# A drain instruction on GpSimd's queue, ahead of the first small expert slot of an attention and mixture-of-experts kernel

## The chip, the cores and the metric

One core of a Trainium2 chip runs the whole program. The metric is the device time of one execution in microseconds (us); lower is better. The core's engines are TensorE (PE, with its weight loads as PEld), VectorE (DVE), ScalarE (ACT), GpSimd (POOL) and SyncE (SP); each works through a queue of instructions of its own, in order.

## The reference, cut to what matters

Attention over 8 batches, 8 heads, 576 tokens and 64 columns with rotary positions, and then a mixture of experts in which each of the 4608 tokens goes to the one expert with the highest gate logit:

```python
attn_out = softmax(rotate(q) @ rotate(k).T / 8) @ v
x = attn_out.transpose(0, 2, 1, 3).reshape(4608, 512)
logits = x @ w_gate
expert_idx = argmax(logits, axis=1)
gate_w = softmax(logits)[arange(4608), expert_idx]
for e in range(8):
    mask = expert_idx == e
    out[mask] = gate_w[mask, None] * (maximum(x[mask] @ w1[e], 0) @ w2[e])
```

## The kernel before, in words

The program has two stages. In the first, which lasts to about 485 us of the span, 32 pairs of heads go through scores, softmax and values in an order that tables at the head of the file set (`PLAN`, `FIRST`, `LAST`). The rows that come out are written to a DRAM buffer (`x_dram`), and the index of every token is scattered to the list of its expert (`xlist`) by indirect DMAs that GpSimd issues (`listed`, line 898).

The second stage works through slots of one expert each. A large slot is 256 tokens, a small slot 128. The number of slots depends on the data, so that both loops stand in nested `tc.If` blocks at the end of the function (lines 1434 to 1441): up to 21 large slots, of which this data uses 17 (`s` from 0 to 16), and up to 8 small ones, of which it uses 6 (`s` from `SB` = 22). `counts` holds the two numbers; every engine loads the second of them at line 1432 and then branches at line 1438.

In a slot, SyncE loads the two weight matrices of the next expert where they change (`reload`), ACT and DVE split them into a high and a low part (`split1`, `split2`), and TensorE multiplies. GpSimd computes nothing in this stage. It only issues the indirect DMAs: in large slots the gathers of rows of a later slot (`gather_pieces`, line 441; for three slots `gather`, line 460), for small slots one gather each (`gather_small`, line 1064), issued as early as the large slots, and in every slot the scatter of finished rows to the output (`out_rows`, line 1198), two for a large slot and one for a small one. The rows wait in a tile `y` with three buffers, which DVE (line 249) or ACT (line 1197) fills.

Where a block of large slots is skipped, its false branch holds, on GpSimd, waits for the landings of all earlier indirect DMAs and one instruction that adds to the semaphores what the skipped DMAs would have added (in the rows it stands as INC_SWDGE_SEM); the same stands in the false branch of the small slots. Behind the last block comes the end of the program, which the rows give line 1544: SyncE waits for all landings, each engine runs a drain and reports to GpSimd, GpSimd runs a drain of its own, takes the four reports and releases all engines; a second such round follows, around a clearing of the semaphores.

`small_slot` is called once per small slot. Its first call of `half` emits the first 12 products on TensorE, and the branch `s == SB` below it is taken for the first small slot alone. Of GpSimd's instructions a small slot has only the scatter at its end.

Of the kernel before, what the change touches and what calls it, by code (L numbers as in the profile page):

```python
# [177 lines left out]
def kernel(  # L178
# [12 lines left out]
    nc = tc.nc  # L191
# [236 lines left out]
    def slot_indices(s):  # L428
        return sib[:, s - SB:s - SB + 1] if s >= SB else gi[s % NG]
# [49 lines left out]
    def take():  # L479

        return pairs.pop(0)

    def give(t):
        pairs.append(t)
# [574 lines left out]
    def blocks(t):  # L1059

        return t.rearrange("p (g q c) -> p g c q", q=P, c=2)
# [7 lines left out]
    def reload(s, which, regs, part=None):  # L1069
        if not regs:  # L1070
            regs.append(reg(s, 1, E - 1))
            regs.append(None if s == 0 else reg(s, 2, 1))
        ev, cv = regs
        kw = {} if cv is None else dict(cond=cv)
        for g in range(FQ) if part is None else [part]:
            if which == 1:
                nc.sync.dma_start(out=r1[g], in_=src1(bass.ds(ev, 1), g, SP0 <= s < SB), **({} if s == SP0 else kw))
            else:
                nc.sync.dma_start(out=r2[g], in_=src2(bass.ds(ev, 1), g), **kw)

    def split(hi, lo, src):
        nc.scalar.copy(out=hi, in_=src)  # L1082
        nc.vector.tensor_tensor(out=lo, in0=src, in1=hi.bitcast(F32), op=ALU.subtract)  # L1083

    def split1(g):
        split(w1h[g], w1l[g], r1[g])

    def split2(g):
        split(w2h[g], w2l[g], r2[g])
# [14 lines left out]
    def quarters(t):  # L1104
        return t.rearrange("p a (b q) -> p (a b) q", q=256)
# [15 lines left out]
    def xturn(s, nj):  # L1121
        src = quarter_rows(rows_of(s))
        ps = take()
        readers[id(ps)] = 2
        for dc in range(DC):
            for j in range(nj):
                nc.tensor.transpose(quarters(ps)[:, dc, j * P:(j + 1) * P], src[:, 4 * j + dc, 0:DQ], ident)
        return ps
# [4 lines left out]
    def xhigh(ps, d2, nj):  # L1133
        sl, w = slice(2 * d2, 2 * d2 + 2), slice(0, nj * P)
        nc.scalar.copy(out=xh[:, sl, w], in_=turned_x(ps)[:, sl, w])

    def xlow(ps, d2, nj):
        sl, w = slice(2 * d2, 2 * d2 + 2), slice(0, nj * P)
        nc.vector.tensor_tensor(out=xl[:, sl, w], in0=turned_x(ps)[:, sl, w], in1=xh[:, sl, w].bitcast(F32),
                                op=ALU.subtract)  # L1140
        if ps is not None:
            both(ps)
# [8 lines left out]
    def relu_parts(hp, w):  # L1151
        hh = hq.tile([P, 2, 256], F32R, name="hh")[:, :, 0:w]
        hl = hq.tile([P, 2, 256], F32R, name="hl")[:, :, 0:w]
        nc.scalar.activation(out=hh, in_=hp, func=AF.Relu)
        nc.vector.scalar_tensor_tensor(out=hl, in0=hp, scalar=0.0, in1=hh.bitcast(F32), op0=ALU.max, op1=ALU.subtract)
        return hh, hl
# [12 lines left out]
    def first_products(fs):  # L1169
        return [(w[dc][:, fs], x[:, dc]) for dc in range(DC) for w, x in ((w1h, xh), (w1l, xh), (w1h, xl))]  # L1170
# [23 lines left out]
    def out_rows(s, t, si, yp, ordered):  # L1194
        y = mp.tile([P, DM], F32, name="y", bufs=3)
        w = weight_of(s, t)
        chained_emit(lambda: nc.scalar.mul(y, yp, w) if t else ts(y, yp, w, ALU.mult), ordered)
        sc = nc.gpsimd.indirect_dma_start(  # L1198
            out=out, out_offset=bass.IndirectOffsetOnAxis(ap=si[:, t:t + 1], axis=0),
            in_=y, in_offset=None, bounds_check=NT - 1, oob_is_err=False)  # L1200
        tc.declare_no_dep(sc.ins, group="out", reason="every row is written once")
        tc.add_to_no_dep_group("out", sc.ins)

    def small_slot(s, last):


        def half(h, at):
            t = take()
            hp = t[:, 0]
            todo = first_products(slice(h * 512, h * 512 + 512))  # L1210
            for i, (w, x) in enumerate(todo):
                nc.tensor.matmul(hp, lhsT=x[:, 0:P], rhs=w, start=(i == 0), stop=(i == len(todo) - 1))
                for f in at.get(i, ()):
                    f()
            return t

        def held(hp):
            hs = mp.tile([P, 512], F32, name="hs", bufs=2)
            nc.scalar.copy(out=hs, in_=hp[:, 0])
            give(hp)  # L1220
            return hs

        def turned(hs):

            tp = take()
            for b in range(FQ):
                nc.tensor.transpose(tp[:, 0, b * P:(b + 1) * P], blocks(hs)[:, b // 2, b % 2], ident)
            return tp

        def rounded(tp):  # L1230
            hh, hl = (t.rearrange("p a (b q) -> p (a b) q", q=P) for t in relu_parts(quarters(tp)[:, 0:2], 256))
            give(tp)
            return [(hh[:, 2 * g:2 * g + 2], hl[:, 2 * g:2 * g + 2]) for g in range(2)]

        def next1(d):
            if not last:
                split1(d)

        hs, hp = [], half(0, {})
        if s == SB:  # L1240
            split2(0)
            split2(1)
            hs.append(held(hp))
            split2(2)
            split2(3)
        else:
            for g in range(1, FQ):
                split2(g)
            hs.append(held(hp))
        parts = []  # L1250

        def first_half():
            tp = turned(hs[0])
            if s > SB:
                next1(0)
            parts.extend(rounded(tp))
            if s == SB:
                next1(0)

        hp = half(1, {5: [first_half]})  # L1260
        next1(1)
        hs.append(held(hp))
        if not last:
            reload(s + 1, 2, regs_of[s])
        ps = None if last else xturn(s + 1, 1)
        yt = take()
        yp = yt[:, 0]

        def second(g):
            hh, hl = parts[g]  # L1270
            for i, (h, w, fi) in enumerate([(hh, w, fi) for fi in range(2) for w in (w2h[g], w2l[g])] +
                                           [(hl, w2h[g], fi) for fi in range(2)]):
                nc.tensor.matmul(yp, lhsT=h[:, fi], rhs=w[:, fi], start=(g == 0 and i == 0),
                                 stop=(g == FQ - 1 and i == 5))

        second(0)
        tp = turned(hs[1])
        if not last:
            xhigh(ps, 0, 1)
            xhigh(ps, 1, 1)  # L1280
            xlow(ps, 0, 1)
            xlow(ps, 1, 1)
            next1(2)
        parts.extend(rounded(tp))
        if not last:
            next1(3)
        for g in range(1, FQ):
            second(g)
        if not last:
            split2(0)  # L1290
        out_rows(s, 0, slot_indices(s), yp, False)
        give(yt)
# [30 lines left out]
    def slot(s, nj):  # L1323
        if s < 3 or s >= NA_MIN:
            chained.clear()
        last = s == SB + NB_MAX - 1
        regs = []
        if s + 1 == S1:
            indices(S1, 2, gi[S1 % NG])
        if s + 1 == S1:  # L1330
            gather(S1, 2)
        if s + 1 >= S1 and s + 2 < SB:
            indices(s + 2, 2, gl[s % 2])
        j = s - S1 - 1
        if 0 <= j < NB_MAX:
            indices(SB + j, 1, sib[:, j:j + 1])
        if 1 <= j <= NB_MAX:
            gather_small(j - 1)
        if not last:
            reload(s + 1, 1, regs)  # L1340
        if nj == 1:
            regs_of[s] = regs
            return keep(lambda: small_slot(s, last))
        hs = []
        mm1(s, hs)
        reload(s + 1, 2, regs)
        xtrans(s + 1)
        mm2(s, hs)
# [199 lines left out]
```

## Time and profile before

| what | value |
|---|---|
| median of 3 runs | 966.09 us (965.85 to 968.06) |
| the profiled execution's own time | 962.38 us |
| span of the profiled execution | 960.6 us |
| time outside the span | 1.78 us |
| granted clock of TensorE, mean | 0.993 |
| TensorE busy | 924.5 us, 96% |
| GpSimd busy | 650.6 us, 68%, 559 instructions |

Times in rows count from the start of the span, in us, and durations in a list by source line are in ns (least, median, most). An engine's name with a q behind it (POOLq, SPq) is its queue: branches, semaphore waits and drains, which are not counted as busy. A time outside the span belongs to the execution but to no instruction.

### The profile page before, as it was taken

Reading aid. Unit: us, or ns where it says so; the run is one execution under the profiler, and the core shown is the slowest. Engines: PE = TensorE matmul, PEld = TensorE weight load, DVE = VectorE, ACT = ScalarE, POOL = GpSimd, SP = SyncE. Lnnn points to the kernel's source line nnn. Section 1 sums busy time; section 2 is a strip of 40 time slices with the busy share of each in tenths; the row PEclk is TensorE's granted clock in tenths of the full one; section 3 lists DMA queues with packets and bytes.
Section 4 is the critical chain, followed back from the end, with each engine's and each line's share of the span. In section 5 each row is a group of like instructions: output and inputs, shape, how many; then the busy total and the mean of one; then the engine's idle time right before and its main releaser. Section 6 shows DMA issues by size and latency. Waiting matters only on the chain.

```text
span 960.6 us, 25200 instructions
## 1 busy us (share of the span) xinstructions
PE 924.5 (96%) x9514; PEld 770.0 (80%) x9514; DVE 754.2 (79%) x1324; ACT 624.7 (65%) x1104; POOL 650.6 (68%) x559
## 2 busy tenths in 40 slices
PE   7899999999999999998899999999999999999994
PEld 6677777777777777776689999999999999996883
DVE  7788878788788878778468677777787788788994
ACT  6887777777777777676454444555455555556883
POOL 2998799999989896976346556767667666553110
PEclk9999999999999999999999999999999999999998
DMA  7785665656647655442711277614416311167970
GB/s 256 231 258 149 188 168 161 174 160 193 183 125 220 173 158 164 140 129 85 233 58 47 76 219 235 196 50 146 148 57 194 97 50 47 44 207 273 383 268 10
DMA packets 65492, 152.61 MB, mean 159 GB/s; under 512 B 18841, under 2 KB 34009, under 8 KB 60368
## 3 DMA queue, kind: packets, MB, share of 16 engines
q1 hardware_dynamic: 55760, 130.67, 44.4%
q0 software_dynamic: 9600, 20.23, 6.7%
q8 instruction: 77, 1.26, 0.6%
q14 instruction: 55, 0.45, 0.2%
HBM read 162.35 MB, written 22.69 MB: 193 GB/s over the span
## 4 chain that ended last, share of the span: by engine, by line
PE 53%; issue 18%; POOL 14%; DVE 6%; ACT 4%; DMA 3%; POOLq 0%; DVEq 0%; SPq 0%; ACTq 0%
PE pb L694 12%; PE pb L605 11%; PE pb L1178 10%; PE pb L1305 9%; POOL xg L441 4%; PE pb L631 4%; DVE PT L563 4%; POOL xt L441 3%; PE pb L736 3%; POOL out_dram L1198 3%; PE pb L699 3%; ACT pn L621 3%; DMA qk<-in_qk_dram 1%; DMA out_dram<-y,gi 1%; ACT PT L563 1%
## 5 line engine op out<-in xcount | busy, mean ns | idle before, releaser
L621 ACT ACTIVATE pn<-pb,negm 128x576 f32<-128x576 f32 x256 | 187.2, 739 | 63.1 <-DVE negm L610 57.2
L610 DVE TENSOR_REDUCE negm<-pb 128x1 f32<-128x576 f32 x288 | 201.4, 747 | 16.9 <-PE pb L605 10.2
L605 PE MATMUL pb<-rK,rX 64*128 64x288 f32 (+1 forms) x960 | 166.2, 310 | 7.5 <-DMA rX<-rQ 4.2
L605 PE MATMUL pb<-rK,rQ 64*128 64x288 f32 (+1 forms) x960 | 166.4, 310 | 3.7 <-DVE lgt L762 0.7
L605 PEld LDWEIGHTS pb<-rK,rX 64*128 64x128 f32 (+1 forms) x960 | 133.4, 181 | 26.4 <-issue 10.2
L694 PE MATMUL pb<-PT,vn 128*64 128x320 f32 (+1 forms) x1024 | 150.2, 412 | 3.8 <-issue 3.4
L1178 PE MATMUL pb<-xh,w1h 128*128 128x256 f32 x544 | 153.8, 283 | 0.0
L1178 PE MATMUL pb<-xh,w1l 128*128 128x256 f32 x544 | 153.7, 283 | 0.0
L1178 PE MATMUL pb<-xl,w1h 128*128 128x256 f32 x544 | 153.7, 283 | 0.0
L605 PEld LDWEIGHTS pb<-rK,rQ 64*128 64x128 f32 (+1 forms) x960 | 133.3, 181 | 12.6 <-DVE PT L563 6.8
L1083 DVE TENSOR_TENSOR w2l<-r,w2h 128x1024 fp32r<-128x1024 f32 x89 | 107.4, 1218 | 30.4 <-ACT w2h L1082 26.0
L441 POOL DMA_INDIRECT xg<-x_dram,gp x64 | 90.9, 1420 | 57.5 <-DVE gp L251 40.0
L563 ACT COPY PT<-pb 128x1024 f32<-128x1024 f32 (+1 forms) x99 | 97.3, 1000 | 35.4 <-PE pb L655 30.3
L441 POOL DMA_INDIRECT xt<-x_dram,gp x56 | 79.5, 1420 | 50.0 <-DVE gp L251 31.3
L694 PEld LDWEIGHTS pb<-PT,vn 128*64 128x64 f32 x1024 | 68.8, 136 | 53.0 <-issue 10.8
L1083 DVE TENSOR_TENSOR w1l<-r,w1h 128x1024 fp32r<-128x1024 f32 x88 | 104.7, 1220 | 2.6 <-ACT w1h L1082 1.9
L1178 PEld LDWEIGHTS pb<-xh,w1h 128*128 128x128 f32 x544 | 106.1, 195 | 0.7
L1178 PEld LDWEIGHTS pb<-xh,w1l 128*128 128x128 f32 x544 | 106.1, 195 | 0.5
L1305 PE MATMUL pb<-w2h,hh 128*128 128x512 f32 x272 | 106.2, 390 | 0.0
L1178 PEld LDWEIGHTS pb<-xl,w1h 128*128 128x128 f32 x544 | 106.1, 195 | 0.0
L1305 PE MATMUL pb<-w2l,hh 128*128 128x512 f32 x272 | 106.0, 390 | 0.0
L1305 PE MATMUL pb<-w2h,hl 128*128 128x512 f32 x272 | 105.9, 389 | 0.0
(227 smaller groups left out, 2021.6 us busy)
## 6 DMA issues: line engine op xcount, KB each, us to landing
r<-in_moe_w_dram SPq DMA_DIRECT2D x136, 512.0 KB
qk<-in_qk_dram SPq DMA_DIRECT2D x31, 1152.0 KB
r<-in_moe_w1q_dram SPq DMA_DIRECT2D x56, 512.0 KB
rX<-rQ SPq DMA_DIRECT2D x128, 144.0 KB
x_dram<-xt SPq DMA_DIRECT2D x8, 1032.0 KB
vn<-in_v_dram SPq DMA_DIRECT2D x32, 256.0 KB
vr<-in_vlast_dram SPq DMA_DIRECT2D x32, 64.0 KB
xlist<-mark SPq DMA_DIRECT2D x3, 408.0 KB
```

What stands on the lines that cost most here:

```text
L441: nc.gpsimd.indirect_dma_start(out=t[:, k], out_offset=None, in_=x_dram.rearrange("n (q w) -> (n q) w", q=4), in_offset=bass.IndirectOffse ...
L563: (nc.scalar.copy if eng == "a" else nc.vector.tensor_copy)(out=o, in_=i)
L605: nc.tensor.matmul(sp[0:m, r, 0:HS], lhsT=st["Q" if r == h else "X"][rows[r], a, cols], rhs=parts(st["K"][rows[r], b])[:, h], start=(a + b ...
L610: nc.vector.tensor_reduce(out=st["negm"][:, j:j + 1], in_=st["S", j][:, :, 0:HS], axis=AX.XY, op=ALU.max, negate=True)
L621: nc.scalar.activation(out=parts(pt), in_=sp[:, :, 0:HS], func=AF.Exp, bias=st["negm"][:, j:j + 1], scale=1.0, accum_out=z)
L631: nc.tensor.transpose(tp[:, r, k * 256 + i * 64:k * 256 + i * 64 + 64], pn[rows[r], i, c:c + P], ident[rows[r], rows[r]])
L694: m = nc.tensor.matmul(to[:, 0:w], lhsT=st["vn"][:, h, kt, :], rhs=st["PT"][:, 4 * h + kt, half * 256:half * 256 + w], start=(kt == 0), st ...
L699: m = nc.tensor.matmul(to[:, 0:w].rearrange("p (i q) -> p i q", i=k), lhsT=vr[n % NVR][:, h], rhs=st["PT"][:, 4 * half:4 * half + k, 576:6 ...
L736: m = nc.tensor.matmul(o[:, r, c * 72:c * 72 + 72], lhsT=st["uT"][rows[r], c * P:(c + 1) * P], rhs=iw[rows[r], n % NP, :], start=True, sto ...
L1083: nc.vector.tensor_tensor(out=lo, in0=src, in1=hi.bitcast(F32), op=ALU.subtract)
L1178: m = nc.tensor.matmul(hp[:, fi], lhsT=w, rhs=x, start=(i == 0), stop=(i == len(todo) - 1))
L1305: m = nc.tensor.matmul(yp[:, t], lhsT=h[:, fi, ts_], rhs=w[:, fi], start=(g == 0 and fi == 0 and i == 0), stop=(g == FQ - 1 and fi == 1 an ...
```

## The change

One instruction is added to GpSimd's queue. In the program's order it stands in the block of the first small slot, behind that block's branch (line 1438) and ahead of the slot's scatter (line 1198, with its register move and its wait). It waits for no semaphore and updates none. On the other four engines, and on GpSimd behind it, instructions and waits are what they were.

```diff
         hs, hp = [], half(0, {})
         if s == SB:
+            nc.gpsimd.drain()
             split2(0)
             split2(1)
             hs.append(held(hp))
```

## Rows read from the trace of the kernel before

**Rows 1.** Stretches: length, busy (instructions) of PE, PEld, DVE, ACT, POOL; clock, DMA, GB/s.
```profile
886.00:947.90 61.90, 60.80 (x296) 50.64 (x294) 58.97 (x65) 50.82 (x68) 8.54 (x6) 1.00 0.72 270
947.90:950.70 2.80, 0.00 (x0) 0.00 (x0) 0.00 (x0) 0.00 (x0) 0.94 (x1) 1.00 0.16 63
950.70:960.60 9.90, 0.00 (x0) 0.00 (x0) 0.00 (x0) 0.00 (x0) 0.00 (x0) 0.52 0.00 0
```

**Rows 2.** Line 1544, instructions between 950 and 951 us.
```profile
L1544 POOLq DRAIN  x1: 9060/9060/9060, 950.7 to 950.7; - x1
```

**Rows 3.** Line 1544, instructions between 951.1 and 959 us, SyncE's drains.
```profile
L1544 SPq DRAIN  x2: 7/10/13, 951.2 to 951.3; - x2
```

**Rows 4.** SyncE's queue after 945 us, whom it waited for (total, times, longest).
```profile
SPq L1544 <- DMA out_dram<-y,sib: 10.8, 1, 10.8
SPq L1544 <- PEq L1544: 9.2, 2, 8.7
```

**Rows 5.** Line 1544, whole span: GpSimd's events and drains, SyncE's events.
```profile
L1544 POOLq EVENT_SEMAPHORE  x4: 17/17/17, 959.8 to 960.5; - x4
L1544 POOLq DRAIN  x3: 51/107/9060, 950.7 to 960.3; - x3
L1544 SPq EVENT_SEMAPHORE  x14: 17/28/28, 950.5 to 960.5; - x14
```

**Rows 6.** Line 1529, the start of the program: GpSimd's drain.
```profile
L1529 POOLq DRAIN  x1: 169/169/169, 0.3 to 0.3; - x1
```

**Rows 7.** GpSimd's groups of indirect DMAs in the whole span.
```profile
L441 POOL DMA_INDIRECT xg<-x_dram,gp x64 | 90.9, 1420 | 57.5 <-DVE gp L251 40.0 <-issue 14.6 <-PE pb L1178 2.9
L441 POOL DMA_INDIRECT xt<-x_dram,gp x56 | 79.5, 1420 | 50.0 <-DVE gp L251 31.3 <-issue 13.1 <-PE pb L1178 5.6
L898 POOL DMA_INDIRECT xlist<-tid,lpi x40 | 45.3, 1133 | 12.0 <-issue 7.4 <-DMA gi<-xlist 3.4 <-DMA x_dram<-xt 0.3
L1198 POOL DMA_INDIRECT out_dram<-y,gi x34 | 40.1, 1180 | 16.5 <-issue 9.1 <-DVE y L249 6.1 <-ACT w2h L1082 0.9
L1064 POOL DMA_INDIRECT xsm<-x_dram,sib x8 | 9.7, 1212 | 2.4 <-issue 2.4
L1198 POOL DMA_INDIRECT out_dram<-y,sib x6 | 9.5, 1579 | 65.8 <-DVE y L249 55.1 <-DVEq L1438 10.7
L460 POOL DMA_INDIRECT xt<-x_dram,gi x4 | 4.7, 1166 | 15.6 <-DVE uT L714 14.7 <-issue 0.9
L460 POOL DMA_INDIRECT xg<-x_dram,gi x4 | 4.6, 1145 | 1.2 <-issue 1.2
```

**Rows 8.** GpSimd's queue at the two false branches (lines 1434 and 1438).
```profile
L1434 POOLq INC_SWDGE_SEM  x1: 2277/2277/2277, 879.2 to 879.2; - x1
...
L1438 POOLq INC_SWDGE_SEM  x1: 2371/2371/2371, 948.1 to 948.1; - x1
```

**Rows 9.** Chain of waits, 868 to 883 us.
```profile
871.27 10.11 DMA out_dram<-y,gi
...
882.07 0.04 POOLq L1438
...
882.15 0.04 POOLq L1198
```

**Rows 10.** GpSimd's timeline, 850 to 961 us.
```profile
872.61 1.00 POOL L1198 DMA_INDIRECT out_dram<-y,gi  x1 [0.31 <-ACT w2h L1082]
886.04 1.70 POOL L1198 DMA_INDIRECT out_dram<-y,sib  x1 [12.44 <-DVE y L249]
898.40 1.70 POOL L1198 DMA_INDIRECT out_dram<-y,sib  x1 [10.65 <-DVE y L249]
```

**Rows 11.** GpSimd's timeline, 474 to 490 us.
```profile
478.21 1.00 POOL L460 DMA_INDIRECT xt<-x_dram,gi  x1 [0.30 <-issue]
479.24 2.37 POOL L1364 TENSOR_TENSOR w1l<-r,w1h 128x1024 fp32r<-128x1024 f32 x1
```

**Rows 12.** Tile y after 880 us, DVE's writes of it.
```profile
L249 DVE TENSOR_SCALAR y<-pb,xsm x6: 751/751/754, 885.0 to 946.8; 128x512 f32<-128x512 f32 x6
```

## The prediction

> **What bounds the kernel now.** TensorE is busy for 96% of the span, so the last place where anything else counts is where TensorE has finished. I therefore read the busy time by stretches first, at the end of the span [rows 1]: up to 947.9 us TensorE is busy for 60.80 of 61.90 us, and the other engines follow it. From there on no engine computes. 2.80 us hold only the issue of the last scatter, and then come 9.90 us in which nothing is busy and no DMA moves anything. The list of the end's instructions says what these 9.90 us are: one drain on GpSimd's queue that starts at 950.7 us and executes for 9060 ns [rows 2], that is to 959.8 us.
>
> Next is the question whether something else would have held the end back anyway. SyncE's waits [rows 4] and its instructions [rows 3, 5] answer it: SyncE waited for the landing of the last scatter, had that by 950.5 us (its first wait for landings is over there, [rows 5]), and had executed its own drain by 951.3 us [rows 3]. From then on it waited 8.7 us; the view puts that down to TensorE's queue, but TensorE had nothing left to do, and SyncE's wait ends when GpSimd, behind its drain, takes the reports (first at 959.8 us, [rows 5]) and releases everyone. So the drain alone sets the end, for all but its first 0.6 us. What follows it, 960.60 - 959.76 = 0.84 us, is the release and the second round.
>
> **What the change adds, and where.** It adds one drain. The chain of waits [rows 9] gives its place: GpSimd's branch into the first small slot is at 882.07 us, the next instruction of the slot at 882.15 us, so the drain starts at about 882.15 us. Queued behind it on GpSimd are the scatter of the first small slot, which now starts at 886.04 us [rows 10] when DVE's y is there, and the five scatters behind that. Ahead of it, the scatters of the last large slot were issued by 873.61 us, and their landings had been waited for in the false branch by 881.38 us [rows 9]. GpSimd stands still for 12.44 us there [rows 10], of which 886.04 - 882.15 = 3.9 us lie behind the drain's start.
>
> *How long the new drain takes.* No row shows a drain in that place. The rows give two ends: 51 to 169 ns for a drain with nothing but a few fills or semaphore instructions ahead of it [rows 5, 6], and 9060 ns for the one at the end, with the whole kernel ahead of it [rows 2]. What lies between the two kinds is the 216 indirect DMAs that GpSimd issued (64 + 56 + 40 + 34 + 8 + 6 + 4 + 4, [rows 7]). The drain at the end can't be waiting for the newest of them: the last scatter had landed by 950.5 us [rows 4, 5] and the semaphore instruction ahead of the drain had ended at 948.1 + 2.37 = 950.5 us [rows 8]. It isn't plain work that lags on GpSimd's cores either: a subtract behind an indirect DMA starts 0.03 us after that DMA's row ends and has an ordinary length [rows 11]. So what the drain executes is either older than the newest work, something that each indirect DMA leaves behind until a drain clears it, or a routine of fixed length.
>
> I take the first: 9060 / 216 = 42 ns for each indirect DMA since the last drain. Then 210 of them are cleared in the middle, at 210 x 42 ns = 8.8 us, from 882.15 to about 891.0 us. The first scatter moves from 886.04 to about 891.1 us, 5 us later, and is issued by 892.8 us, 5.6 us before the second is due at 898.40 us [rows 10]. The cover is GpSimd's own idle time. Nobody reads the output in the kernel; the one who waits for a scatter is DVE, which fills y again when the scatter three slots earlier has landed. DVE's six fills stand 12.36 us apart ((946.8 - 885.0) / 5, [rows 12]), so the fourth, at 922.1 us, needs the first scatter landed; with the slow landing of this stretch, 10.11 us from the issue [rows 9], it has landed at 901.2 us, 21 us in time. Without that cover the 5 us would fall on DVE and then on TensorE. The price of the added drain on the path is therefore 0.
>
> *What goes.* The drain at the end then has 6 scatters ahead of it, 6 x 42 ns = 0.25 us, and the floor of 0.05 to 0.17 us seen for empty ones. It would be over at about 951.0 us, and SyncE's drain, over at 951.3 us [rows 3], is late next. The end moves from 959.76 to about 951.29 us: **8.5 us less**. If the drain keeps a fixed part of a few us besides the 42 ns, it saves less: with half of 9.06 us kept, the drain ends at 955.4 us and 4.4 us go.
>
> *The sum.* Span 960.6 - 8.5 = 952.1 us; with the 1.78 us around it the profiled execution would take 953.9 instead of 962.38 us. The runs shown have a median 3.7 us above that execution, and I put the same 8.5 us on the median: 966.09 - 8.5 = **957.6 us**. Taken alone, this case reaches from 956.0 (the least run lies 0.2 us under the median, and the empty drain may add a few tenths of saving in the release) to 962.0 us (half of the length kept).
>
> **The rule that speaks against it.** The rows show drains of 7 to 13 ns on SyncE [rows 3] and of 51 to 9060 ns on GpSimd [rows 5]. The Trainium skill, "VectorE: DVE Perf Modes", section "The DRAIN you can't avoid", says that the drains from a program's beginning and end are boilerplate of about 12 ns, constant, on all five engines. By that rule the added drain costs 12 ns, the one at the end isn't something to save, and the time stays at 966.1 us. The trace agrees for SyncE and not for GpSimd's row of 9060 ns.
>
> **The rivals.**
>
> *The drain has a fixed length once indirect DMAs have run (chance 0.34).* For it: only one drain with indirect DMAs ahead of it is in the trace, so one length can't tell 42 ns each from 9.06 us at once; the instruction that adds to semaphores also takes much the same in both places, 2277 and 2371 ns, however many DMAs lie between [rows 8]. Against it: nothing that the rows show was open at 950.7 us. Then the middle drain takes 9.06 us, hidden as above, and the one at the end again 9.06 us, since six scatters and a semaphore instruction lie between. The time is 966.1 us.
>
> *The added drain doesn't do what the one at the end does (0.06).* Its queue is empty at 882.15 us, and if the length belongs to the last semaphore instruction or to the place at the program's end, the new one takes 0.05 to 0.17 us and leaves the 9.06 us where they are: 966.1 us.
>
> *The drain in the middle takes so long that y runs out (0.04).* The 9060 ns were measured with the DMA engines still [rows 1]. At 882 us they are loaded: a landing that is over within the 2.80 us stretch at the end [rows 1] took 10.11 us there [rows 9]. If the drain grew by the same ratio it would take 9.06 x 10.11 / 2.80 = 32.7 us, to 914.9 us. The first scatter would then land at about 915 + 1.7 + 10.1 = 926.7 us, while DVE wants its buffer at 922.1 us: DVE, and TensorE behind it, would stand for 4.6 us. This decides from a drain of about 28 us on. If the end also keeps its 9.06 us, the time is 966.1 + 4.6 = 970.7 us.
>
> **How the numbers follow.** A measurement of this kernel can tell about 0.3% (2.9 us) from no change, so faster means under 963.2 and slower over 969.0 us. The forecast gets 0.56, because the length of the drain goes with what GpSimd's queue has issued in all the rows that there are, and because the newest work was over; it doesn't get more, because a single long row stands for that. The two cases of no change get 0.34 + 0.06 = 0.40, the slower one 0.04. The likeliest time is 957.6 us. To hold 8 in 10 the range must take in the forecast and the unchanged cases: from 956.0 us to 968.0 us, which is 966.1 us and the highest run shown.
>
> **What would show it.** Right: a drain at line 1241 of the changed kernel at about 882 us with some 8.8 us, the first small scatter at about 891 us and the second at its old place, a drain at the end well under 1 us, and SyncE no longer waiting behind its own drain. The fixed length shows as two drains of about 9 us. The idle drain shows as one under 0.2 us in the middle and 9.06 us at the end. The forecast is wrong wherever the last drain stays above some 6 us.

## The result, and the profile after

The changed kernel takes 958.29 us, the median of 6 runs (955.35 to 961.67), and the kernel before, run beside it, 966.17 us (6 runs, 965.42 to 968.06). The ratio is 0.9916, with a 95% interval from 0.9895 to 0.9938: 7.9 us less, which the interval bounds at 6.0 and 10.1 us. The forecast was 957.6 us, within 956.0 to 968.0 us.

The first thing to look at is the end of the span, where the saving was expected. Stretches of the changed kernel (length, busy time and instructions of PE, PEld, DVE, ACT, POOL; clock, DMA share, GB/s):

```profile
889.70:951.60 61.90, 60.76 (x296) 50.61 (x294) 58.92 (x65) 51.00 (x69) 8.74 (x6) 1.00 0.73 274
951.60:955.80 4.20, 0.00 (x0) 0.00 (x0) 0.00 (x0) 0.00 (x0) 0.90 (x1) 0.84 0.11 42
```

The small slots run as before: TensorE is busy for 60.76 us of the 61.90 (60.80 before, [rows 1]), with the same 296 instructions. Behind them there are 4.20 us without computing, where there were 2.80 + 9.90 us. To compare more exactly I call the time from the end of DVE's last write of `y` to the end of the span the tail. It was 960.60 - 947.59 = 13.0 us and is 955.79 - 951.25 = 4.54 us, 8.47 us shorter.

The drains and the semaphore instructions of GpSimd, from the lists of three source lines (line 1241 is the change, 1439 the false branch of the small slots, 1545 the end; ns, least/median/most, then first and last start):

```profile
L1241 POOLq DRAIN  x1: 8570/8570/8570, 885.7 to 885.7; - x1
L1435 POOLq INC_SWDGE_SEM  x1: 2278/2278/2278, 882.8 to 882.8; - x1
L1439 POOLq INC_SWDGE_SEM  x1: 295/295/295, 951.8 to 951.8; - x1
L1545 POOLq DRAIN  x3: 51/113/2152, 952.3 to 955.5; - x3
```

A long drain now stands in the middle, 8570 ns from 885.7 us, and the one at the end has gone from 9060 [rows 2] to 2152 ns. The semaphore instruction ahead of it fell as well, from 2371 [rows 8] to 295 ns, which the prediction had not thought of.

GpSimd's timeline shows what the middle drain moved (start, length, instruction, and in brackets the idle time before it):

```profile
876.26 1.00 POOL L1198 DMA_INDIRECT out_dram<-y,gi  x1 [0.30 <-ACT w2h L1082]
895.16 1.85 POOL L1198 DMA_INDIRECT out_dram<-y,sib  x1 [17.90 <-DVE hl L1155]
902.06 1.71 POOL L1198 DMA_INDIRECT out_dram<-y,sib  x1 [5.04 <-DVE y L249]
...
951.52 0.97 POOL L1198 DMA_INDIRECT out_dram<-y,sib  x1 [10.67 <-DVEq L1439]
```

In this execution everything from the later large slots on lies 3.65 us later than before (the last large scatter at 876.26 instead of 872.61, [rows 10]). The first small scatter is at 895.16 instead of 886.04 + 3.65 = 889.69 us, so 5.5 us late; the second is at 902.06, and 898.40 + 3.65 = 902.05: back in place. The drain used up idle time and nothing else.

At the end, the instructions of line 1545 on SyncE and whom SyncE waited for (total, times, longest):

```profile
L1545 SPq EVENT_SEMAPHORE  x14: 17/28/2126, 952.0 to 955.7; - x14
L1545 SPq DRAIN  x3: 7/7/13, 954.9 to 955.2; - x3
```

```profile
SPq L1545 <- DMA out_dram<-y,sib: 10.8, 1, 10.8
SPq L1545 <- PEq L1545: 0.7, 2, 0.5
```

SyncE's wait for the last landing now lasts until 952.04 + 2.13 = 954.17 us, GpSimd's drain ends at 952.28 + 2.15 = 954.44, and SyncE's own drain comes at 954.9 us. SyncE waited 9.2 us behind it before [rows 4] and 0.7 us now. So GpSimd is done first and SyncE sets the end.

The profiled execution took 957.57 us with a span of 955.8, only 4.8 us less than before's 962.38 and 960.6, though its tail is 8.47 us shorter. The other 3.66 us were lost ahead of the change, about half of them some 400 us ahead of it: ACT's instructions start 0.87 us later than before at 448 us, 2.8 us later at 473 us and 3.64 us later at 679 us. Two stretches there, of the changed kernel and then of the kernel before:

```profile
440.00:460.00 20.00, 16.34 (x216) 12.42 (x212) 13.03 (x32) 10.68 (x25) 11.92 (x36) 0.90 0.48 131
460.00:485.00 25.00, 23.23 (x246) 15.25 (x248) 12.40 (x20) 11.09 (x19) 7.11 (x6) 0.87 0.56 204
```

```profile
440.00:460.00 20.00, 15.49 (x218) 11.44 (x215) 13.44 (x31) 10.96 (x25) 12.67 (x37) 1.00 0.47 122
460.00:485.00 25.00, 23.36 (x267) 15.86 (x265) 12.56 (x22) 11.69 (x19) 7.49 (x6) 1.00 0.57 204
```

TensorE's granted clock was 0.90 and 0.87 there instead of 1.00, and 246 instead of 267 products fit into the second stretch. From 460 to 465 us it was 0.50, the lower of its two levels (1.2 and 2.4 GHz), with TensorE busy for 3.50 of the 5.00 us ahead of that. In the execution before, TensorE was busy for 3.71 us of the same 5.00 and the clock stayed at 1.00. The instructions are the same in both kernels at that point, so this belongs to the one execution and not to the change. The same changed kernel, profiled again on another chip (e11 below), has other clocks in these stretches:

```profile
440.00:460.00 20.00, 16.96 (x214) 13.62 (x212) 14.00 (x33) 12.12 (x28) 13.15 (x36) 0.83 0.48 152
460.00:485.00 25.00, 25.00 (x294) 18.63 (x291) 14.09 (x23) 14.32 (x21) 11.06 (x6) 1.00 0.47 170
```

It is why the medians of six runs, not the two profiles' spans, carry the verdict.

### The profile page after: what moved, and what is told of

Same layout as the page of the kernel before. It is cut to its first block, busy times and chain, and to the rows that moved or that the text cites. A ratio compares the mean times of both kernels' runs of the same rounds, so it can differ in the third digit from the quotient of the medians.

```text
span 955.8 us, 25201 instructions
## 1 busy us (share of the span) xinstructions
PE 927.9 (97%) x9514; PEld 771.8 (81%) x9514; DVE 755.8 (79%) x1324; ACT 626.1 (66%) x1104; POOL 647.3 (68%) x559
## 4 chain that ended last, share of the span: by engine, by line
PE 52%; issue 18%; POOL 15%; DVE 6%; DMA 4%; ACT 2%; POOLq 1%; DVEq 0%; SPq 0%; ACTq 0%
PE pb L694 11%; PE pb L605 11%; PE pb L1178 10%; PE pb L1306 9%; POOL xg L441 4%; PE pb L631 4%; DVE PT L563 4%; POOL xt L441 3%; POOL out_dram L1198 3%; PE pb L736 3%; PE pb L699 3%; DMA qk<-in_qk_dram 3%; ACT pn L621 2%; DMA out_dram<-y,gi 1%; DVE negm L610 1%
```

## The experiments

The drain at the end shrank to less than a quarter, but 2152 ns are not the 0.25 us of the forecast. So the question was what a GpSimd drain costs and why. The theories, by the letters that the expectations use: **L**, the forecast's, 42 ns for each indirect DMA since the last drain (41 in the expectations, 8570 / 210); **F**, a fixed price paid once; **I**, a price for each instruction of GpSimd since the last drain; **W**, added in the second run, a drain waits until the newest indirect DMA has landed; **K**, which came out of the runs themselves, described where it does. The other letters are explained where they come.

Three chips were used, one for e1 to e4, one for e6 to e9 and one for e10 and e11, each with the kernel before beside them. Its medians there were 958.18 us (e1 to e4; 7 runs, 956.79 to 960.26), 957.22 us (e6 to e9; a single run) and 957.08 us (e10, e11; 11 runs, 955.98 to 959.07). Where a time is from a single run it is called so.

In e1, e4 and e6 to e9 a drain is held in its place in GpSimd's queue, behind a chosen instruction `m`, by an order-only dependency:

```python
def drain_behind(m):
    d = nc.gpsimd.drain()
    tc.add_manual_dep(
        d.ins, m.name, mybir.DependencyInfo(mybir.DependencyClass.NoSync, mybir.DependencyReason.DATA),
        reason="the drain's place")
    return d.ins
```

### e1_three_places: two more drains, early

```diff
     listed_steps(FIRST)
+    chained_emit(lambda: nc.gpsimd.drain(), True)
...
     route_rest()
-    nc.gpsimd.memset(xsm, 0.0)
+    d_ = drain_behind(rows_first[0])
+    m_ = nc.gpsimd.memset(xsm, 0.0)
+    place_behind(m_.ins, d_)
```

> Three drains: behind the first list of steps of the attention stage (2 indirect DMAs and about 110 other GpSimd instructions ahead of it), ahead of the filling of xsm at the change of stages (41 more indirect DMAs and some 330 more other instructions), and at the first small slot as in the change (167 more). Theory L, the drain clears something that every indirect DMA since the last drain has left, about 41 ns each (8570 ns / 210): under 0.3, then 1.7, then 6.8 us, and the one at the end ends some 0.3 us behind the last landing. Theory F, the first drain behind indirect DMAs pays a fixed price once in the execution: 8.6 us at the first drain, under 0.3 us at the second and third. Theory I, every GpSimd instruction leaves something, 9060 / 559 = 16 ns: about 1.8, then 5.9, then 2.7 us. The tail behind the last write of y is 4.5 us as with the change in all three.

One run took 949.77 us. The three added drains, in the lists of their lines:

```profile
L1023 POOLq DRAIN  x1: 1712/1712/1712, 133.6 to 133.6; - x1
L1011 POOLq DRAIN  x1: 8027/8027/8027, 506.9 to 506.9; - x1
L1254 POOLq DRAIN  x1: 5038/5038/5038, 877.2 to 877.2; - x1
```

The first has 2 indirect DMAs and 91 other instructions of GpSimd ahead of it, the second 41 and 247, the third 167 and 1. F is out: the price isn't paid once, and it differs. I is out: 1 other instruction goes with 5038 ns and 91 with 1712. The first drain missed L's under 0.3 us, but its row begins when the queue reaches it: GpSimd's last computing instruction ahead of it ran until 135.10 us, and the drain ended at 135.36, 0.26 us behind. L has the direction but not the size: 167 x 41 ns = 6.8 us were expected at the small slots and 5.04 were measured. The second drain does not fit L at all (41 x 41 ns = 1.7 us, measured 8.03), but the last landing that the trace has for the DMAs ahead of it is at 513.25 us, and it ended at 514.98 us, 1.72 us behind that landing.

### e2_slot14: one drain, while DMAs are under way

```diff
     def slot(s, nj):
+        if s == 14:
+            nc.gpsimd.drain()
...
         if s == SB:
-            nc.gpsimd.drain()
```

> One drain, not at the first small slot but at the beginning of large slot 14, with 180 indirect DMAs ahead of it and 36 behind it. Theory L: 180 x 41 ns = 7.4 us there, and at the end 36 x 41 ns = 1.5 us behind the last landing; SyncE needs 0.8 us behind that landing anyway, so the tail behind the last write of y is some 0.7 us longer than with the change (5.2 instead of 4.5 us). Theory F: 8.6 us there, and a tail of 4.5 us. Theory that the length is fixed for each drain behind indirect DMAs is out already. If GpSimd's idle time in slot 14 doesn't cover the drain, TensorE stands still in slots 14 to 16, where it had no gap of over 0.2 us; I expect none.

One run took 949.67 us. Its drains, and SyncE's wait at the end:

```profile
L1325 POOLq DRAIN  x1: 8687/8687/8687, 798.7 to 798.7; - x1
L1546 POOLq DRAIN  x3: 51/107/3004, 944.0 to 947.6; - x3
```

```profile
SPq L1546 <- PEq L1546: 1.7, 2, 1.1
```

The middle drain delayed nothing that TensorE needs; the stretch around it:

```profile
797.00:808.00 11.00, 11.00 (x93) 11.00 (x93) 7.89 (x20) 6.35 (x8) 3.30 (x4) 1.00 0.19 62
```

The middle drain was expected to take 7.4 us by L and 8.6 by F. It took 8.69, but landings were outstanding: it ended 3.08 us behind the last of them. The drain at the end had 36 DMAs ahead of it and took 3004 ns in all, 83 ns for each. It ran until 1.75 us behind the last landing, where L had 1.5, SyncE waited longer for it (1.1 instead of 0.5 us at most), and the tail was 5.49 us (5.2 by L, 4.5 by F) instead of 4.52. So F is out here too, and a drain at the end costs something again when it has a few tens of DMAs left.

### e3_each_small: a drain at every small slot, and two in a row at the first

```diff
         hs, hp = [], half(0, {})
+        nc.gpsimd.drain()
         if s == SB:
             nc.gpsimd.drain()
```

> Two drains in a row at the first small slot and one at the beginning of each later one, so that each has one scatter ahead of it and the one at the end has one too. Theory L: 8.6 us and then under 0.2 us at the first slot, under 0.2 us at the later ones (their scatter has landed long before), and at the end the drain ends within 0.1 us of the last landing instead of 0.3 us; since SyncE is later than that, the time is that of the change, 958 us. Theory F: the same at the start, and no shorter end. Theory R, what the end has left after the change (2.15 us) is a fixed rest of a drain: 2 us at each of the later small slots.

The median of 4 runs is 949.72 us (948.15 to 950.13), a ratio of 0.9905 (0.9885 to 0.9925) to the kernel before on that chip. The drains:

```profile
L1240 POOLq DRAIN  x6: 3159/6824/8570, 878.7 to 931.6; - x6
L1242 POOLq DRAIN  x1: 40/40/40, 887.3 to 887.3; - x1
```

The pair at the first slot is 8570 and then 40 ns: the first clears everything, and a drain with nothing to do is nearly free, in this place too. The five in the later slots were a miss. Each was expected under 0.2 us because the scatter ahead of it would have landed long before. But the drain's queue reaches it right behind that scatter, and the five rows have 6807, 6885, 6247, 6842 and 3159 ns, each ending 0.07 to 0.08 us after its scatter's landing. One DMA can't cost 6.8 us to clear; the drains were waiting for landings. The drain at the end, with one scatter ahead of it, ended 0.08 us behind the last landing, as L has it.

### e4_behind_scatter: a drain right behind each small scatter

```diff
         tc.add_to_no_dep_group("out", sc.ins)
+        if s >= SB:
+            drain_behind(sc.ins)
```

> The drain of the change, and one right behind the scatter of each small slot (the first five stand there; that of the last executed slot comes behind the semaphore instruction of the false branch). Theory W, a drain also waits until the newest indirect DMA has landed: each of these takes what is left of the landing, 3 to 6 us (2 us behind the last one), and none is on the path. Theory N, it doesn't wait for data: under 0.3 us each, and the 2.15 us that the change leaves at the end are not the landing.

One run took 948.15 us. The drains behind the scatters, and those of the end:

```profile
L1011 POOLq DRAIN  x6: 2431/6884/7501, 885.6 to 942.4; - x6
L1559 POOLq DRAIN  x3: 45/55/107, 945.0 to 946.1; - x3
```

They end 0.07 to 0.08 us after the landings, from 2431 ns at the quiet end of the kernel to 7501 ns among weight loads: W holds, with landings longer than the 3 to 6 us expected. With the last scatter drained, the drain of the program's end is down to about 0.05 us, and the tail is still 4.52 us. This is the least that a drain can do for this kernel: below it SyncE sets the end.

### e6 to e9: the length against the count

The four kernels keep the change and add one drain behind the second scatter of a large slot, so that the drain at the small slots has a chosen number of DMAs since the last one: 50, 82, 104 and 126. All of them have landed when it starts, since the false branch ahead of it waits for their landings.

```diff
         tc.add_to_no_dep_group("out", sc.ins)
+        if s == 11 and t == 1:
+            drain_behind(sc.ins)
```

(e6; with 8, 6 and 4 in the place of 11 in e7, e8 and e9.)

> The drain of the change, with an extra drain behind the last scatter of large slot 11, so that 50 indirect DMAs lie between the two, all landed before the second. How does a drain's length go with that number? Theory P, one price for each: 41 ns (8570 / 210), so 2.1 us. Theory K, 79 ns for each (3004 ns / 38 at the end of the run with the drain in slot 14), and in long stretches about 105 of them are cleared on the way without a drain (169 gave 5.04 us, 210 gave 8.57, 216 gave 9.06, which is 79 to 80 ns for each above 105, 102 and 103): 4.0 us. Both: a tail of 4.5 us behind the last write of y, and a time like that of the change.

> The same with the extra drain behind the last scatter of large slot 8, so that 82 indirect DMAs lie ahead of the drain of the change. Theory P: 82 x 41 ns = 3.4 us. Theory K: 82 x 79 ns = 6.5 us, if clearing on the way begins later than that.

> The same behind large slot 6: 104 indirect DMAs. Theory P: 4.3 us. Theory K: 104 x 79 ns = 8.2 us if nothing has been cleared on the way, near 0 if about 105 have just been; anything between speaks against K's steps of 105.

> The same behind large slot 4: 126 indirect DMAs. Theory P: 5.2 us. Theory K: (126 - 105) x 79 ns = 1.7 us if some 105 have been cleared on the way, 126 x 79 ns = 10.0 us if that begins only above 126.

The times, single runs: 949.66, 949.13, 950.27 and 948.10 us, all with a tail of 4.52 us. The drain at the small slots in e6, e7, e8 and e9:

```profile
L1249 POOLq DRAIN  x1: 4157/4157/4157, 877.2 to 877.2; - x1
```

```profile
L1249 POOLq DRAIN  x1: 6770/6770/6770, 876.8 to 876.8; - x1
```

```profile
L1249 POOLq DRAIN  x1: 8567/8567/8567, 879.5 to 879.5; - x1
```

```profile
L1249 POOLq DRAIN  x1: 1707/1707/1707, 874.6 to 874.6; - x1
```

The first three lie on one line, 83, 83 and 82 ns for each DMA. The fourth falls off it: 126 DMAs take 1.7 us, a fifth of what 104 take. This is the reading that decides between P and K, and it is K: **a drain costs about 82 ns for each indirect DMA that has not been cleared, and without any drain about 105 of them are cleared at a time on the way**. By the rate, 1707 ns are 21 DMAs, so 105 of the 126 had been cleared. (The expectation of e6 counts 38 and 169 DMAs where the order of GpSimd's queue gives 36 in e2 and 167 in e1; hence its 79 ns for what the table gives as 82.) All the drains with many DMAs ahead and everything landed:

| kernel | DMAs since the last drain | drain, ns | left, at 82 ns | cleared on the way | INC_SWDGE_SEM ahead, ns |
|---|---|---|---|---|---|
| e6 | 50 | 4157 | 51 | none | 1184 |
| e7 | 82 | 6770 | 83 | none | 1824 |
| e8 | 104 | 8567 | 104 | none | 2271 |
| e9 | 126 | 1707 | 21 | 105 | 584 |
| e1 | 167 | 5038 | 61 | 106 | 1404 |
| change | 210 | 8570 | 105 | 105 | 2278 |
| before (end) | 216 | 9060 | 110 | 106 | 2371 |

The last column agrees by another instruction: the semaphore instruction in the false branch takes about 20 ns for each DMA left, (2271 - 584) / (104 - 21) = 20 ns, and 160 to 190 ns besides.

The drains that these kernels add in the large slots (7578, 7732, 13760 and 13452 ns) have landings outstanding, and none of them made the kernel slower.

The traces hold one thing more. Where landings are outstanding, a drain ends behind the newest landing by about 41 ns for each DMA left, half of the 82: by 0.08 us with 1 left (e3, e4), 0.29 with 6 (the change), 0.87 with 20 or 21 (e10), 0.96 with 22 left of 128 (e7, slot 8), 1.72 with 41 (e1), 3.08 with 74 left of 180 (e2, slot 14) and 3.49 with 84 (e9, slot 4). It looks as if half of the clearing were done ahead of the wait and half behind it; where the first half outlasts the landing, the price is again 82 to 83 ns for each: 3004 ns for the 36 at the end of e2, and for the drains added in e6 and e8, counted from the end of the last DMA's row, 4.49 us with 54 left of 160 and 8.74 us with 106. No run was made to test this.

### e10_more_dmas: no drain, but more DMAs

K says something that the forecast's rule excludes: the end of the kernel before should become short if it had 16 indirect DMAs more, since a second hundred would then be cleared on the way. e10 is the kernel before with 16 gathers into a tile that nobody reads, at the place of the change. It computes all that the reference does.

```diff
+    spare = cpool.tile([P, 16, 4], F32, name="spare")
...
         if s == SB:
+            for k in range(16):
+                nc.gpsimd.indirect_dma_start(
+                    out=spare[:, k], out_offset=None, in_=x_dram.rearrange("n (q w) -> (n q) w", q=129),
+                    in_offset=bass.IndirectOffsetOnAxis(ap=sib[:, 0:1], axis=0),
+                    bounds_check=129 * NT - 1, oob_is_err=False)
```

> The kernel before, without any added drain, but with 16 more indirect DMAs (16 bytes to each partition, into a tile that nobody reads) at the beginning of the first small slot: 232 instead of 216. Theory K, some 105 are cleared on the way each time that more than about that many have piled up, and a drain pays 82 ns for each that is left: 216 left 9060 / 82 = 110, 232 would leave 126, which the drain at the end of the run from slot 4 on showed to be cleared to 21; so the last drain shortens to about the landing of the last scatter, the tail is 4.5 us and the time is that of the change, 8 us less than before, by adding work. Theory C, only a drain clears, or the clearing on the way comes once: 126 x 82 ns = 10.3 us at the end, 1.3 us more than before.

The median of 4 runs is 949.74 us (949.55 to 953.09), a ratio of 0.9931 (0.9911 to 0.9951). At its end:

```profile
L1444 POOLq INC_SWDGE_SEM  x1: 587/587/587, 943.7 to 943.7; - x1
L1550 POOLq DRAIN  x3: 51/113/2674, 944.5 to 947.7; - x3
```

```profile
SPq L1550 <- PEq L1550: 0.8, 2, 0.5
```

With 232 DMAs in place of 216 the drain is 2674 instead of 9060 ns, and the semaphore instruction takes 587 ns, much as e9's 584 with 21 left, so that about 211 had been cleared, twice 105 or 106. K holds, and the rival named beside it (C) falls. The clearing on the way also goes by the number of DMAs and not by time or bytes: the 16 came in the same stretch of time as the last six of the kernel before, and each moves only 16 bytes to a partition. The tail is 4.58 us, and the kernel is as fast as the change on the same chip, without any drain. The 16 gathers delayed the first small scatter to 908.63 us, later than the change does, and that cost nothing either: DVE's six fills of `y` are spaced as before, (942.7 - 880.9) / 5 = 12.36 us.

### e11_change_again: the change on the same chip

No edit: the changed kernel again.

> The change itself on the same chip: drain of 8.6 us at the first small slot, tail of 4.5 us, ratio to the kernel before 0.991 (8.5 of 958 us).

The median of 6 runs is 949.81 us (948.55 to 953.49), a ratio of 0.9926 (0.9908 to 0.9943).

```profile
L1241 POOLq DRAIN  x1: 8570/8570/8570, 878.3 to 878.3; - x1
L1545 POOLq DRAIN  x3: 51/113/2127, 944.1 to 947.3; - x3
```

The middle drain has the same 8570 ns to the nanosecond, the end 2127 ns, and the tail is 4.52 us. The change, e3 and e10 come to the same time within their intervals, and e4's empty end drain has no shorter tail: what was to be had at the end has been had, and no version here is shown to beat the change.

## Why the prediction was right

The time alone says little, because the stated range held the forecast and the case of no change both; the rows decide. By the prediction's steps:

- **The drain alone sets the end: right.** With the drain shortened, the tail lost 8.47 us, and the forecast had 960.6 - 952.1 = 8.5 us. All the other kernels agree: whatever shortened that drain brought a tail of 4.5 to 4.6 us (5.49 in e2).
- **SyncE is late next: right.** Its drain at 954.9 us follows GpSimd's end at 954.44. That is why it makes no difference whether GpSimd's last drain takes 2152 ns (the change) or some 0.05 us (e4).
- **The place of the added drain: right.** Forecast 882.15, measured 885.70 us in an execution that runs 3.65 us late, so 882.05.
- **It is hidden in GpSimd's idle time, and the price on the path is 0: right.** The second scatter is in place, and TensorE's busy time in the small slots is 60.76 against 60.80 us.
- **Its length: 8.57 us for a forecast of 8.8, but by a wrong rate.** This is the mis-sized term: "42 ns for each indirect DMA since the last drain". The rate is 82 ns for each DMA not yet cleared, and about half of the 216 had been cleared on the way (e6 to e9). That the length came out is luck: the two errors cancelled because 210 leaves 105 and 216 leaves 110. With 126 DMAs the prediction's rule gives 5.3 us, and e9 has 1.7. The saving didn't hang on the rate, only on the drain at the end having little left. One row can be divided by any count that stands beside it; that the quotient is a rate needed a second count.
- **The end drain: forecast 0.25 us, measured 2.15.** The sign that was named for it, well under 1 us, did not come. A term is missing, put at nothing: the drain waits for the newest landing (W). Before, the semaphore instruction of 2.37 us ended only with the landing and hid that wait; it shrank to 0.30 us, so the drain now begins while the last scatter is still under way, and ends 954.44 - 954.17 = 0.3 us behind its landing. Since SyncE waits for the same landing, it costs nothing.
- **"The drain at the end can't be waiting for the newest of them": right for that row**, where the landing was over. As a statement about drains it would have been wrong, as e3 and e4 show.
- **The range's lower bound: not what its terms give.** 957.6 less the 0.2 us and the few tenths named for it is about 957, not 956.0 us. The result lies above both.

The rivals: the **fixed length** is out: one kernel has drains of 40 and of 8570 ns, and seven counts give lengths from 1.7 to 9.06 us. What stood for it, two semaphore instructions of much the same length, follows from K: they had 104 and 110 DMAs left. That the **added drain does nothing** is out by its 8570 ns and by the end's fall from 9060 to 2152. The rule that the prediction quotes against itself from the Trainium skill ("VectorE: DVE Perf Modes", section "The DRAIN you can't avoid"), drains of about 12 ns on all engines, holds here for SyncE's 7 to 13 ns and not for GpSimd's drain at the end, 9060 ns before and 2152 with the change. That rule speaks of the drains at a program's beginning and end, so the 12 ns for the added one were the prediction's own step. The **long drain** came nearest in the large slots, with 13.8 us in e8 where landings were outstanding. It stayed under the 28 us from which it would decide.

Left open: what is cleared, where between 110 and 126 DMAs not yet cleared the clearing on the way begins, and what it costs when it comes. No row shows that cost: 105 DMAs at 82 ns would be 8.6 us, but from 530 us on no indirect DMA of the kernel before takes over 2.0 us, and none of e10's 16 gathers over 2.1. A long drain without any cover, in the middle of the kernel, wasn't tried either; the end of the kernel before is the only uncovered one here.

## What to carry to other kernels

Read the stretch behind the last computing instruction as carefully as the computing: a drain of 9 us stood there, and the list of the end's instructions names it at once. Before you shorten such a wait, look for who would be ready without it, since that bounds the gain (here SyncE, 8.5 us). Where the cost depends on work piled up on a queue, it can be paid early, in idle time of that engine, with little work queued behind the payment; and before a length is made a rate, measure it at several counts.

## What the runs showed of the hardware that was not expected

- The cost of a drain on GpSimd is not monotonic in the number of indirect DMAs: 104 take 8567 ns and 126 take 1707. Hence 16 useless DMAs make this kernel 0.7% faster (e10).
- A drain on GpSimd waits for landings: with a single scatter ahead of it, it took 2431 to 7501 ns and ended 0.07 to 0.08 us after the landing (e4). With 6 and 36 DMAs, part of the clearing ran beside that wait: 0.3 us (the change) and 1.75 us (e2) were left behind the landing.
- The semaphore instruction in a false branch took from 203 ns with 1 DMA left (e3) to 2371 ns with 110 (before), [rows 8].
